# Two column pieces per held output tile: the end of a retention and feed-forward kernel on one core

## The chip, the cores and the metric

The kernel runs on one core of a Trainium2 chip. The metric is the device time of one execution in microseconds (us). Before the change the median of three runs is 618.58 us, from 618.2 to 619.4.

## The reference

A block-wise retention (attention with decay) over q, k, v of 2 x 8 heads x 768 positions x 64 gives x of 1536 tokens x 512. Two feed-forward layers follow:

```python
    x = np.ascontiguousarray(attn_out.transpose(0, 2, 1, 3)).reshape(B * S, H * D)
    h = x @ w_in
    g = np.where(h >= 1, h, np.where(h <= -1, 0.0, (h + 1) ** 2 / 4))
    x = g @ w_out
    return (x @ w_a * (x @ w_b)) @ w_out2
```

w_in is 512 x 2048, w_a and w_b are 512 x 1536, and the last matrix is 1536 x 512. The change concerns the end of that last product alone.

## The kernel before, in words

Tokens are worked on in three blocks of 512 (nb = 0, 1, 2). All large products go through `mm3` (line 354): every operand is kept as a rounded high part and a low part, both in float32r, and a product of one 128-wide slice is three matmuls (high x high, high x low, low x high) that add into one PSUM bank of 128 x 512 f32. Each matmul has its own load of 128 x 128 weights before it.

The second layer runs over six groups g of 256 hidden features, two feature tiles (`fts`) each. For each group `both_banks` makes the products of x with w_a and w_b and multiplies them, and `o_stage` (line 509) then multiplies with the last matrix: for each of the four row tiles m = 0 to 3 of a token block it calls `o_bank` (line 489), which issues 2 x 3 = 6 matmuls of 512 columns. For the blocks nb = 0 and 1, and for m = 0 of nb = 2, the sum over the groups is kept in SBUF: `gather` (line 464) adds the bank to it on VectorE, and the last group's sum is stored as a whole from the SP queue (line 499). For m = 1, 2, 3 of nb = 2 three PSUM banks are set aside, so that the sum stays in PSUM over all six groups:

```python
    for m in range(1, KT):
        held[m] = banks.popleft()
```

The last call of the kernel is `o_stage(groups - 1, 2, 2)` (line 662). There TensorE has the six matmuls of m = 0, then those of m = 1, 2, 3; VectorE adds m = 0; then each held bank goes out in two halves of 256 columns: VectorE copies the first into an SBUF buffer `o` and SP's queue stores it, ScalarE copies the second and its own queue stores that (lines 504 to 507). Nothing is left to do on any engine after m = 3 but its copies and stores.

The program is written out in the order in which each engine executes it; there is no planner that reorders. The framework places the waits (semaphores) between engines from what each instruction reads and writes. An engine takes its instructions in order, so that an instruction that waits holds up all that is behind it on its engine.

Of the kernel before, what the change touches and what calls it, by code (L numbers as in the profile page):

```python
# [22 lines left out]
DM = H * D  # L23
# [12 lines left out]
def retention_ffn_kernel(ctx: ExitStack, tc: tile.TileContext, lam, att, w1i, w1o, w2ab, w2o, out):  # L36
# [7 lines left out]
    nc = tc.nc  # L44
# [16 lines left out]
    def bank():  # L61
        banks.rotate(-1)
        return banks[-1]
# [3 lines left out]
    def t2(name):  # L67
        return two.popleft()
# [282 lines left out]
            bg()  # L351


    def mm3(ps, pairs, start=True, stop=True):
        n = len(pairs)
        for i, (l, r) in enumerate(pairs):
            for j, (a, b) in enumerate(((0, 0), (0, 1), (1, 0))):
                nc.tensor.matmul(out=ps, lhsT=l[a], rhs=r[b],   # L358
                                 start=(start and i == 0 and j == 0), stop=(stop and i == n - 1 and j == 2))

    def product_in(kind, ft, nb):

        ps = bank()
        w, x = wt[kind, ft], xy[nb]
        mm3(ps, [([w[:, a, k * 128:(k + 1) * 128] for a in range(2)], [x[k][:, b] for b in range(2)])
                 for k in range(KT)])
        return ps
# [45 lines left out]
    def both_banks(ft):  # L413
# [7 lines left out]
        def prod(w, x):  # L421
            ps = bank()
            mm3(ps, list(zip(w, x)))
            return ps
# [33 lines left out]
    def gather(total, ps, first):  # L458

        if first:  # L460
            total = t2("acc")
            nc.scalar.copy(total, ps)
        else:
            nc.vector.tensor_tensor(out=total, in0=total, in1=ps, op=ALU.add)  # L464
        return total

    def y_bank(g, nb, m, last):
        ps = bank()
        fts = range(4 * g, 4 * g + 4)
        mm3(ps, [([wt["1o", f][:, a, m * 128:(m + 1) * 128] for a in range(2)],  # L470
                  [gt[1, f, nb][:, b, :] for b in range(2)]) for f in fts])
        y = acc["y", nb, m] = gather(acc.get(("y", nb, m)), ps, g == 0)
        if last:
            xy[nb] = [block[nb][:, k] for k in range(KT)]
            if nb != 1 or m >= 2:
                split_act(y, xy[nb][m][:, 0], xy[nb][m][:, 1])
            if nb == 2:
                free2(acc.pop(("y", nb, m)))
# [8 lines left out]
    held = {}  # L487

    def o_bank(g, nb, m, last):
        fts = range(2 * g, 2 * g + 2)  # L490
        r0 = nb * TB + m * 128
        pairs = [([gt[2, f, nb][:, a, m * 128:(m + 1) * 128] for a in range(2)],
                  [wt["2o", f][:, b] for b in range(2)]) for f in fts]
        if m not in held or nb < NB - 1:
            ps = bank()
            mm3(ps, pairs)
            o = acc["o", nb, m] = gather(acc.get(("o", nb, m)), ps, g == 0)
            if last:
                nc.sync.dma_start(out=out[r0:r0 + 128], in_=o)
            return  # L500
        mm3(held[m], pairs, g == 0, last)
        if last:
            o = t2("o")
            for i, copy, queue in ((0, nc.vector.tensor_copy, nc.sync), (1, nc.scalar.copy, nc.scalar)):
                cols = slice(i * DM // 2, (i + 1) * DM // 2)
                copy(o[:, cols], held[m][:, cols])
                queue.dma_start(out=out[r0:r0 + 128, cols], in_=o[:, cols])

    def o_stage(g, nb, pieces):
        last = g == FF2 // 256 - 1  # L510
        for m in range(KT):
            o_bank(g, nb, m, last)
            bg(pieces)
        for f in range(2 * g, 2 * g + 2):
            four.append(gt.pop((2, f, nb)))
            if nb == NB - 1:
                four.append(wt.pop(("2o", f)))
# [113 lines left out]
    for i in range(2, len(stages)):  # L631
        g, nb = stages[i]
# [76 lines left out]
```

## Time and profile before

| what | us |
|---|---|
| median of three runs (lowest, highest) | 618.58 (618.2, 619.4) |
| span of the profiled execution, its only given time | 618.3 |
| TensorE busy | 597.7 (97%) |
| VectorE busy | 457.3 (74%) |
| GpSimd busy | 278.5 (45%) |
| ScalarE busy | 267.8 (43%) |

One execution was profiled. Busy time is the sum of the spans of an engine's instructions; matmuls are pipelined and their ends are modelled, so two that follow each other overlap in the records, and the distance of their starts is what one costs. In the profile PE is TensorE (PEld its weight loads), DVE VectorE, ACT ScalarE, POOL GpSimd, and SPq and ACTq are the DMA issues of SyncE and ScalarE. The page's chain follows the work that ended last back from the end, at each step to what released it. Tiles have the names of the program: `ps` is a PSUM bank, `four` and `late_four` are split operands, `two` and `late_two` are 128 x 512 f32 buffers in SBUF, which `o` is one of.

### The profile page before, as it was taken

How to read it: one execution, taken by the hardware profiler on the slowest of the kernel's cores; microseconds unless marked ns; L12 is line 12 of the kernel's file. 1: busy time of each engine (PE TensorE's matmuls, PEld its weight loads, DVE VectorE, ACT ScalarE, POOL GpSimd, SP SyncE). 2: the span in 40 equal slices, each digit the busy share in tenths (PEclk: the TensorE clock that was granted, in tenths of full speed). 3: DMA queues.
4: the chain of work that ended last, by engine and by line, in shares of the span. 5: the costliest groups of instructions: out<-in, count | busy, mean ns of one | idle time of the engine just before them, and what ended most of it. 6: DMA issues, size and time to landing. Idle time of an engine off the chain costs nothing.

```text
span 618.3 us, 8380 instructions
## 1 busy us (share of the span) xinstructions
PE 597.7 (97%) x3100; PEld 488.4 (79%) x3100; DVE 457.3 (74%) x684; ACT 267.8 (43%) x473; POOL 278.5 (45%) x218
## 2 busy tenths in 40 slices
PE   7797899999999999999999999999999999999997
PEld 3676678888888888888888788888888888888886
DVE  1578861964975786497869997989979979979553
ACT  1245552655642553264545456434424424424110
POOL 3535570443522543352947655553453553543420
PEclk9799899999999999999999999999999999999999
DMA  5965520221310212131101222302302202300004
GB/s 176 378 247 203 184 92 1 75 96 68 103 64 10 98 68 69 34 103 49 55 1 35 68 87 83 103 34 90 95 21 96 92 18 93 100 14 1 0 23 182
DMA packets 20937, 52.72 MB, mean 85 GB/s; under 512 B 2584, under 2 KB 4896, under 8 KB 20896
## 3 DMA queue, kind: packets, MB, share of 16 engines
q1 hardware_dynamic: 19624, 51.52, 24.3%
q10 hardware_dynamic: 1272, 0.67, 0.4%
q8 instruction: 24, 0.39, 0.3%
q14 instruction: 17, 0.14, 0.1%
HBM read 49.03 MB, written 3.15 MB: 84 GB/s over the span
## 4 chain that ended last, share of the span: by engine, by line
PE 82%; DVE 8%; ACT 4%; POOL 2%; issue 2%; DMA 1%; ACTq 0%; DVEq 0%; POOLq 0%
PE ps L358 79%; DVE words L294 1%; PE ps L225 1%; PE ps L221 1%; DVE two L302 1%; DVE words L298 1%; DVE two L401 1%; DMA lamp<-in_lam 1%; ACT words L280 1%; DVE two L311 1%; PE ps L150 1%; DVE two L180 1%; DMA rows<-base 1%; ACT four L265 1%; ACT two L281 0%
## 5 line engine op out<-in xcount | busy, mean ns | idle before, releaser
L266 POOL TENSOR_TENSOR four<-two,four 128x512 fp32r<-128x512 f32 x109 | 143.1, 1319 | 213.6 <-ACT four L265 203.4
L358 PE MATMUL ps<-block,four 128*128 128x512 f32 x828 | 196.9, 391 | 1.4 <-POOL block L266 1.4
L358 PEld LDWEIGHTS ps<-block,four 128*128 128x128 f32 x828 | 154.6, 188 | 35.4 <-POOL block L266 1.8
L358 PE MATMUL ps<-four,four 128*128 128x512 f32 x633 | 162.0, 389 | 0.0
L358 PEld LDWEIGHTS ps<-four,four 128*128 128x128 f32 x633 | 118.7, 188 | 24.9 <-issue 0.2
L265 ACT CAST four<-two 128x512 fp32r<-128x512 f32 x109 | 67.1, 620 | 93.4 <-DVE two L451 23.7
L266 POOL TENSOR_TENSOR late_four<-two,late_four 128x512 fp32r<-128x512 f32 x47 | 62.2, 1329 | 56.8 <-ACT late_four L265 49.5
L358 PE MATMUL ps<-block,late_four 128*128 128x512 f32 x324 | 77.2, 389 | 0.0
L358 PEld LDWEIGHTS ps<-block,late_four 128*128 128x128 f32 x324 | 60.8, 188 | 12.6
L280 ACT ACTIVATE words<-raw 128x512 f32<-128x512 f32 x68 | 43.1, 634 | 55.0 <-DVE two L302 49.7
L358 PE MATMUL ps<-four,late_four 128*128 128x512 f32 x243 | 64.0, 389 | 0.0
L377 ACT ACTIVATE two<-two,half 128x512 f32<-128x512 f32 x42 | 30.2, 720 | 70.4 <-DVE two L376 70.4
L294 DVE TENSOR_SCALAR words<-words 128x512 f32<-128x512 f32 x68 | 47.0, 691 | 17.4 <-ACT words L280 17.4
L358 PE MATMUL ps<-late_four,four 128*128 128x512 f32 x213 | 58.5, 389 | 0.0
L358 PEld LDWEIGHTS ps<-four,late_four 128*128 128x128 f32 x243 | 45.6, 188 | 9.5
L464 DVE TENSOR_TENSOR two<-two,ps 128x512 f32<-128x512 f32 x62 | 42.2, 680 | 13.1 <-PE ps L358 13.1
L311 DVE CUSTOM_DVE_ANT_0 two<-two,two 128x1024 uint16<-128x1024 uint16 x54 | 49.7, 921 | 1.9
L376 DVE TENSOR_SCALAR two<-ps 128x512 f32<-128x512 f32 x42 | 28.7, 684 | 29.9 <-PE ps L358 29.4
L298 DVE TENSOR_SCALAR words<-words 128x512 int32<-128x512 int32 x68 | 47.5, 699 | 2.3
L426 DVE TENSOR_TENSOR two<-two,ps 128x512 f32<-128x512 f32 x50 | 32.9, 682 | 19.2 <-PE ps L358 16.7
L358 PEld LDWEIGHTS ps<-late_four,four 128*128 128x128 f32 x213 | 40.0, 188 | 8.3
L265 ACT CAST late_four<-two 128x512 fp32r<-128x512 f32 x47 | 28.9, 620 | 36.4 <-DVE two L440 11.4
(99 smaller groups left out, 596.3 us busy)
## 6 DMA issues: line engine op xcount, KB each, us to landing
load<-in_att SPq DMA_DIRECT2D x48, 256.0 KB, 5.3
raw<-in_w2ab SPq DMA_DIRECT2D x24, 512.0 KB, 3.2
raw<-in_w1i SPq DMA_DIRECT2D x16, 512.0 KB, 3.4
raw<-in_w1o SPq DMA_DIRECT2D x16, 512.0 KB, 3.3
raw<-in_w2o SPq DMA_DIRECT2D x12, 512.0 KB, 3.2
out<-two SPq DMA_DIRECT2D x7, 256.0 KB, 2.0
dmask<-rows SPq DMA_DIRECT2D x2, 256.0 KB, 4.6
out<-late_two SPq DMA_DIRECT2D x2, 256.0 KB, 2.0
```

The lines of the kernel that those rows point to most:

```text
L150: nc.tensor.matmul(out=sc[c][h % 2][:, pr * CH:(pr + 1) * CH], lhsT=kT[p0:p0 + 64, pr * CH:(pr + 1) * CH], rhs=qT[p0:p0 + 64, pr * CH:(pr ...
L265: nc.scalar.copy(hi, src)
L266: (engine or nc.gpsimd).tensor_tensor(out=lo, in0=src, in1=hi.bitcast(F32), op=ALU.subtract)
L280: nc.scalar.activation(out=words, in_=r[:, :, 1].bitcast(F32), func=ACTF.Abs)
L294: nc.vector.tensor_scalar(out=words, in0=words, scalar1=HIGH_MIN, scalar2=HIGH_MAX, op0=ALU.max, op1=ALU.min)
L298: nc.vector.tensor_scalar(out=word, in0=word, scalar1=3, scalar2=0x3FFFFFFF, op0=ALU.logical_shift_left, op1=ALU.bitwise_and)
L311: nc.vector.tensor_tensor(out=v, in0=v, in1=c, op=ALU.add)
L358: nc.tensor.matmul(out=ps, lhsT=l[a], rhs=r[b], start=(start and i == 0 and j == 0), stop=(stop and i == n - 1 and j == 2))
L376: nc.vector.tensor_scalar(out=r, in0=ps, scalar1=-1.0, scalar2=1.0, op0=ALU.max, op1=ALU.min)
L377: nc.scalar.activation(out=r, in_=r, func=ACTF.Square, scale=0.5, bias=half)
L426: add = lambda o, x, ps: nc.vector.tensor_tensor(out=o, in0=x, in1=ps, op=ALU.add)
L464: nc.vector.tensor_tensor(out=total, in0=total, in1=ps, op=ALU.add)
```

## The change

For the held tiles of the last group the six matmuls of 512 columns are replaced by two runs of six: first over the first columns of the bank, then over the rest. For m = 1 the pieces are 256 and 256 columns wide, for m = 2 and 3 they are 384 and 128. The copy and the store of a piece stand right behind its matmuls in the program: VectorE and SP's queue for the first piece, ScalarE and its queue for the second. The groups before the last are issued as they were. `skip_group_check` is an option of the program's builder and issues nothing.

```diff
-    def mm3(ps, pairs, start=True, stop=True):
+    def mm3(ps, pairs, start=True, stop=True, **kw):
...
-                                 start=(start and i == 0 and j == 0), stop=(stop and i == n - 1 and j == 2))
+                                 start=(start and i == 0 and j == 0), stop=(stop and i == n - 1 and j == 2), **kw)
...
-        mm3(held[m], pairs, g == 0, last)
-        if last:
-            o = t2("o")
-            for i, copy, queue in ((0, nc.vector.tensor_copy, nc.sync), (1, nc.scalar.copy, nc.scalar)):
-                cols = slice(i * DM // 2, (i + 1) * DM // 2)
-                copy(o[:, cols], held[m][:, cols])
-                queue.dma_start(out=out[r0:r0 + 128, cols], in_=o[:, cols])
+        if not last:
+            mm3(held[m], pairs, g == 0, False)
+            return
+        o = t2("o")
+        at0 = 0
+        for i, width in enumerate({1: (256, 256)}.get(m, (384, 128))):
+            cols = slice(at0, at0 + width)
+            at0 += width
+            mm3(held[m][:, cols], [(l, [r[b][:, cols] for b in range(2)]) for l, r in pairs],
+                False, True, skip_group_check=i > 0)
+            copy, queue = ((nc.vector.tensor_copy, nc.sync), (nc.scalar.copy, nc.scalar))[i]
+            copy(o[:, cols], held[m][:, cols])
+            queue.dma_start(out=out[r0:r0 + 128, cols], in_=o[:, cols])
```

## Rows read from the trace of the kernel before

**Rows 1.** The core: span in us and mean granted TensorE clock.

```profile
core 0: 618.3 us, clock 0.991
```

**Rows 2.** The page's chain that ended last: shares of the span by line.

```profile
PE ps L358 79%; DVE words L294 1%; PE ps L225 1%; PE ps L221 1%; DVE two L302 1%; DVE words L298 1%; DVE two L401 1%; DMA lamp<-in_lam 1%; ACT words L280 1%; DVE two L311 1%; PE ps L150 1%; DVE two L180 1%; DMA rows<-base 1%; ACT four L265 1%; ACT two L281 0%
```

**Rows 3.** The chain in order of time from 609: start us, us, what.

```profile
609.00 5.68 PE ps L358 x25
```

**Rows 4.** Timeline, TensorE: start us, us, line, form, xcount; m = 3 alone.

```profile
613.14 0.84 PE L358 MATMUL ps<-late_four,four 128*128 128x512 f32 x3
613.82 0.84 PE L358 MATMUL ps<-four,four 128*128 128x512 f32 x3
```

**Rows 5.** Timeline from 610.5, other engines; in brackets the idle time before and its releaser.

```profile
610.62 0.69 DVE L464 TENSOR_TENSOR two<-two,ps 128x512 f32<-128x512 f32 x1 [0.68 <-PE ps L358]
...
613.41 0.42 DVE L506 COPY two<-ps 128x256 f32<-128x256 f32 x1 [0.94 <-PE ps L358]
...
613.86 1.66 SPq L507 DMA_DIRECT2D out<-two  x2
613.87 0.37 ACT L506 COPY two<-ps 128x256 f32<-128x256 f32 x1 [0.99 <-DVE two L506]
...
614.70 0.42 DVE L506 COPY two<-ps 128x256 f32<-128x256 f32 x1 [0.87 <-PE ps L358]
615.16 0.37 ACT L506 COPY two<-ps 128x256 f32<-128x256 f32 x1 [0.92 <-DVE two L506]
615.56 0.34 ACTq L507 DMA_DIRECT2D out<-two  x1
```

**Rows 6.** Groups of instructions, 610 to 619: busy us, mean ns of one, idle before.

```profile
L358 PE MATMUL ps<-four,four 128*128 128x512 f32 x12 | 3.4, 389 | 0.0
...
L506 DVE COPY two<-ps 128x256 f32<-128x256 f32 x2 | 0.8, 424 | 1.8 <-PE ps L358 1.8
L506 ACT COPY two<-ps 128x256 f32<-128x256 f32 x2 | 0.7, 372 | 1.9 <-DVE two L506 1.9
```

**Rows 7.** Groups of the whole span: 512 columns out of PSUM, VectorE and ScalarE.

```profile
L376 DVE TENSOR_SCALAR two<-ps 128x512 f32<-128x512 f32 x42 | 28.7, 684 | 29.9 <-PE ps L358 29.4 <-POOL block L266 0.6
...
L428 ACT COPY two<-ps 128x512 f32<-128x512 f32 x10 | 5.8, 582 | 5.5 <-PE ps L358 5.5
```

**Rows 8.** Timeline: VectorE's masks, and the weight loads that wait for the second.

```profile
52.44 1.28 DVE L180 TENSOR_TENSOR two<-ps,dmask 128x512 f32<-128x512 f32 x2
...
53.77 0.31 PEld L225 LDWEIGHTS ps<-two,load 128*64 128x64 f32 x6
```

**Rows 9.** Two weight loads after a wait (timeline), and the group of one.

```profile
56.95 0.30 PEld L358 LDWEIGHTS ps<-block,four 128*128 128x128 f32 x2
...
L358 PEld LDWEIGHTS ps<-four,four 128*128 128x128 f32 x10 | 1.9, 188 | 0.4
```

**Rows 10.** Matmuls of 128 columns: timeline, and ns min/median/max of the line.

```profile
28.91 1.09 PE L225 MATMUL ps<-two,load 128*64 128x128 f32 x16
...
L225 PE MATMUL ps<-two,load x192: 272/273/475, 18.2 to 95.2; 128*64 128x128 f32 x192
```

**Rows 11.** Stores of the last 18 us: xcount, KB each, median us to landing.

```profile
out<-two SPq DMA_DIRECT2D x7, 256.0 KB, 2.0
...
out<-two ACTq DMA_DIRECT2D x2, 128.0 KB, 1.7
```

**Rows 12.** Windows: us, busy by engine PE PEld DVE ACT POOL, PEclk, DMA share, GB/s.

```profile
54.00:58.00 4.00, 2.52 (x34) 1.83 (x31) 3.88 (x6) 1.08 (x2) 3.53 (x3) 1.00 0.82 305
...
62.00:66.00 4.00, 1.23 (x12) 1.23 (x14) 3.84 (x6) 1.88 (x4) 2.72 (x4) 0.79 0.58 176
66.00:68.00 2.00, 2.00 (x22) 1.67 (x20) 1.75 (x3) 0.80 (x2) 1.26 (x1) 0.56 0.90 295
```

**Rows 13.** Timeline of TensorE: the longest idle time before the second clock drop.

```profile
64.77 1.97 PE L221 MATMUL ps<-two,st 64*64 64x128 f32 x16 [4.62 <-POOL two L172]
```

## The prediction

> **What bounds the kernel now.** I read first the clock of the core [rows 1], then the chain that ended last on the page [rows 2], then the same chain over the last nine microseconds [rows 3], and then the last stage instruction by instruction. The chain is TensorE's line 358 for 79% of the span, at a clock of 0.991; so nearly every microsecond that TensorE stands still is a microsecond of the kernel. In the last stage TensorE is one unbroken piece until 614.68, then come a VectorE copy, a ScalarE copy, and the last store. This stage is all that the change touches: the products of earlier groups into held banks are issued as before, and taking the output buffer a little earlier costs nothing, since no engine issues anything for it.
>
> Each of the four output tiles has six matmuls here. Tile m=3 is the last two rows of TensorE's timeline, three matmuls each, which begin at 613.14 and 613.82; so one matmul of 512 columns costs 0.68/3 = 0.227 us and a tile 1.36 [rows 4]. Of these, 512 columns at 2.4 GHz are 0.213, so some 0.014 is spent per matmul. After the last tile's first matmul (613.14) VectorE starts its copy 1.56 later, ScalarE its copy 2.02 later, and the last store is issued 2.42 later, at 615.56 [rows 5]. The store lands 1.7 later, at 617.3, and 1.0 us of closing work ends the span at 618.3.
>
> The row that decides is ScalarE's copy. It reads other columns of the bank than VectorE's copy and writes other columns of the output buffer, yet in both rows it starts 0.03 to 0.04 us after VectorE's ends, and the bracket of its row names VectorE as the releaser [rows 5]. It is not the output buffer that makes it wait: at 613.87 it writes that buffer while the store issued from it at 613.86 has just begun, and does not wait for that. What the two copies share beyond it is the PSUM bank. I read from this that the program orders accesses of different engines to a bank by bank, not by columns.
>
> **The change, part by part.** For each held tile it puts 12 matmuls in place of 6: six on the first columns (piece A), six on the rest (piece B). Between them stands VectorE's copy of A. If the bank is the unit of order, B's first matmul writes the bank that this copy is reading, so it waits for the copy; TensorE takes its work in order, so the next tile's matmuls wait behind it. The cover that hid the copy in the kernel before (the next tile's six matmuls) is gone, three times.
>
> The length of the stall, by rows. The last matmul of a 512-column tile is modelled at 0.389 and VectorE starts 0.04 after its end (613.82 + 0.84 = 614.66, to 614.70) [rows 4 to 6]; for 256 columns I take 0.389 less 0.107 for the missing columns, 0.28; for 384 columns 0.34. VectorE's copy of 256 columns takes 0.424 [rows 6]; of 512 columns out of PSUM an operation takes 0.684, so 384 columns come to 0.55, half way [rows 7]. ScalarE takes 0.372 for 256 [rows 6] and 0.582 for 512 [rows 7], so 0.27 for 128. From the end of a VectorE operation to the weight load that waited for it I find 0.05 (53.72 to 53.77) [rows 8]. One full weight load keeps the following load waiting 0.30 - 0.188 = 0.11 [rows 9], and the first matmul needs its weights, so 0.11 more before B streams.
>
> A matmul of 256 columns I cost at 256/2.4 GHz + 0.014 = 0.12, of 384 at 0.174; the load's 0.11 still fits under both. Not so for 128 columns, where the stream would be 0.067 but the load needs 0.11. The trace has no such matmul: 128 columns are seen only with unrounded f32 operands and 64-wide weights, 16 in 1.09 us, (1.09 - 0.273)/15 = 0.054 each, two halves of the array in turn and two instructions for each product [rows 10]. Those share the column count, but not the operand type and not the whole array. Line 358 shares both, and bounds the cost from above at 0.227, its cost for 512 columns. The lower bound is the weight load, 0.11. The value is nearer to neither row, so I take the middle, 0.17, and keep both ends for the range. TensorE: Matmul & The Clock Gate of the Trainium skill, section Back-to-back issue gap, gives 81 ns for a sustained load and matmul of 128 columns; by that the sum below would be about 1.0 lower, at 2.4. No run here shows its figure, and for 512 columns it has 131 ns where rows 4 have 227.
>
> Counted from each tile's first matmul:
> m=1 (256+256): the last of A starts at 5 x 0.12 = 0.60, ends by the model at 0.88, VectorE starts at 0.92 and ends at 1.35 (it is free: its addition for m=0 ends at 611.31, this would start at 611.35 [rows 5]); the load comes at 1.40, B streams from 1.51, and the next tile begins 6 x 0.12 later, at 2.24. Before: 1.36. **+0.88.**
> m=2 (384+128): A's last start 0.87, end 1.21, copy 1.25 to 1.80, load 1.85, B from 1.96, next tile at 1.96 + 6 x 0.17 = 2.98. **+1.62** (0.11: +1.26; 0.227: +1.96).
> m=3: B's last matmul starts at 1.96 + 5 x 0.17 = 2.81, modelled at 0.31 (between 0.23 and 0.39), ScalarE's copy starts at 3.16, takes 0.27, and the store is issued 0.03 later, at 3.46, against 2.42. **+1.04** (+0.66; +1.41). VectorE's copy is no longer before ScalarE's here, but it has moved in front of the matmuls instead.
> Last store: 64 KB in place of 128. A store of 256 KB lands in 2.0 and one of 128 in 1.7 [rows 11]; I take **-0.1**, with -0.3 and 0 as ends. SP's larger store of m=3 is issued some 1.6 us before ScalarE's and is home first; the number of stores on each queue is unchanged.
> Sum: 0.88 + 1.62 + 1.04 - 0.1 = **+3.4** (2.7 with the narrow matmuls at 0.11, 4.1 at 0.227). On the profiled execution, whose only given time is its span, that is 618.3 + 3.4 = 621.7; this execution lies 0.3 under the median of the three runs (618.58), so the forecast is **622.0**.
>
> On the wait itself: what rows 5 show is reader against reader. PSUM — Partial Sum Buffer of the Trainium skill, section PSUM bank collisions raise a hardware error, asks for the same guard between a matmul's write and a reader, even at other columns of the bank. No row here shows that pair; by the page the sum stands as it is, and without it the first rival holds.
>
> **The rivals.**
> No slower than can be measured: B doesn't wait, because a matmul's write is ordered against a read by columns. What speaks for it is that stores and copies of one output buffer are ordered so [rows 5]. What speaks against it is ScalarE's copy, which waits with no column in common. Then m=1 costs 12 x 0.12 - 1.36 = +0.08, m=2 6 x 0.174 + 6 x 0.17 - 1.36 = +0.70, and in m=3 ScalarE would start at 1.04 + 0.85 + 0.31 + 0.04 = 2.24 and the store be issued at 2.54, +0.12; with -0.1, +0.8 in all: 619.4. With narrow matmuls at 0.11 it is +0.08 + 0.34 - 0.25 - 0.1 = +0.1: 618.7. It decides at the first matmul of B: the point is whether that starts before VectorE's copy ends.
> Slower still: the stalls let TensorE's clock fall. It did fall, from 2.4 to 1.2 GHz for a while, after TensorE had stood still for 4.62 us before 64.77 (granted 0.79 and 0.56 of full in the windows from 62 to 68); from 54 to 58, busy for 2.52 of 4 us, it was granted 1.00 throughout [rows 12, 13]. After the change I work out idle gaps under 0.8 us in the timeline, with TensorE busy about three quarters of the time, so I expect no fall. If it does fall, the columns of m=2's B and m=3 cost twice: 6 x 0.17 + 6 x 0.174 + 5 x 0.17 = +2.9 at most, 624.9 at worst, near 624 if the fall comes with m=3.
> A third, within the forecast: the narrow matmuls at either end, 621.3 or 622.7.
>
> **How the numbers follow.** Forecast with its two ends 82%, B not waiting 12%, the clock falling 6%. The unknowns of the forecast are the narrow matmuls (-0.7, +0.7), the 384-column copies (0.13 each way, twice), VectorE's start after the matmuls (in the stream it is 0.11 after the modelled end, not 0.04: +0.07 three times) and the store (-0.2, +0.1): 620.8 to 623.4 if all go one way. The page's 81 ns would give 621.0. I widen that a little for launch-to-launch scatter (618.2 to 619.4) and for part of the clock's rival: **620.3 to 623.6**. About 0.2%, 1.2 us, is what a measurement of this kernel can tell from no change. Slower by more than that: the forecast, the clock, and a small part of the first rival, 88%. Within it: the rest of that rival, 10%. Faster by more would need 1.2 us out of a tail whose two copies last 0.8 together: 2%.
>
> **What would show it right or wrong.** In the timeline of the last stage: TensorE no longer one piece but with three gaps of some 0.5 to 0.8 us, each ended by VectorE's copy; the first matmul of each B just after that copy's end; six narrow matmuls in 0.7 to 1.4 us; ScalarE's last copy waiting for TensorE, not VectorE; the chain ending TensorE, VectorE, TensorE, ScalarE. The tiles' starts should lie 2.2 and 3.0 apart, not 1.36. The forecast is wrong if B's matmuls begin while VectorE still copies A, or if the granted clock is under 1.00 before the last matmul.

## The result, and the profile after

The changed kernel takes 622.12 us (median of 12 runs, 620.66 to 625.33) where the kernel before takes 618.14 (median of 12, 617.83 to 621.05). The ratio is 1.0056, with a 95% interval of 1.0038 to 1.0074: slower by 3.5 us, between 2.3 and 4.6. The lowest runs are 2.8 apart.

The last stage of the changed kernel, TensorE's timeline (start us, us, line, form, xcount, in brackets the idle time before and its releaser), where [rows 4] had the last of one unbroken piece:

```profile
612.89 0.52 PE L358 MATMUL ps<-late_four,four 128*128 128x256 f32 x3
613.25 0.52 PE L358 MATMUL ps<-four,four 128*128 128x256 f32 x3
614.35 0.62 PE L358 MATMUL ps<-late_four,four 128*128 128x256 f32 x3 [0.58 <-DVE late_two L512]
614.81 0.52 PE L358 MATMUL ps<-four,four 128*128 128x256 f32 x3
615.17 0.69 PE L358 MATMUL ps<-late_four,four 128*128 128x384 f32 x3
615.69 0.68 PE L358 MATMUL ps<-four,four 128*128 128x384 f32 x3
617.10 0.55 PE L358 MATMUL ps<-late_four,four 128*128 128x128 f32 x3 [0.72 <-DVE two L512]
617.49 0.50 PE L358 MATMUL ps<-four,four 128*128 128x128 f32 x3
617.82 0.74 PE L358 MATMUL ps<-late_four,four 128*128 128x384 f32 x3
618.40 0.69 PE L358 MATMUL ps<-four,four 128*128 128x384 f32 x3
619.74 0.55 PE L358 MATMUL ps<-late_four,four 128*128 128x128 f32 x3 [0.65 <-DVE two L512]
620.13 0.49 PE L358 MATMUL ps<-four,four 128*128 128x128 f32 x3
```

VectorE and ScalarE in the same stretch, to be held against [rows 5]:

```profile
613.10 0.69 DVE L464 TENSOR_TENSOR two<-two,ps 128x512 f32<-128x512 f32 x1 [0.67 <-PE ps L358]
613.87 0.42 DVE L512 COPY late_two<-ps 128x256 f32<-128x256 f32 x1
616.49 0.56 DVE L512 COPY two<-ps 128x384 f32<-128x384 f32 x1 [2.19 <-PE ps L358]
619.12 0.56 DVE L512 COPY two<-ps 128x384 f32<-128x384 f32 x1 [2.08 <-PE ps L358]
```

```profile
620.66 0.27 ACT L512 COPY two<-ps 128x128 f32<-128x128 f32 x1 [2.37 <-PE ps L358]
620.95 0.34 ACTq L513 DMA_DIRECT2D out<-two  x1
```

Before each second piece stands a gap, and its bracket names VectorE's copy of the first piece: the copy of 616.49 ends at 617.05, the next weight load and matmul begin at 617.10. ScalarE's last copy now waits for TensorE, where it waited for VectorE. The tiles' first matmuls lie 2.27 and 2.65 us apart (612.89, 615.17, 617.82), where they were 1.36.

The changed stretch by itself, from m=1's first matmul to the end of the span, took 618.31 - 610.42 = 7.89 us before and 623.54 - 612.89 = 10.65 after: **+2.76**. m=1 of the kernel before begins here:

```profile
610.42 0.84 PE L358 MATMUL ps<-late_four,four 128*128 128x512 f32 x3
```

The rest of the distance of the two profiled spans lies ahead of that stretch, where both kernels issue the same instructions: m=1 begins 2.47 later after the change (612.89 against 610.42). The chain of each profile (start us, us, what) shows that this distance is there in full when the attention stage ends and the long run of 984 matmuls begins, the kernel before first:

```profile
0.73 4.93 DMA lamp<-in_lam
95.51 223.28 PE ps L358 x984
```

```profile
0.73 6.48 DMA lamp<-in_lam
97.98 223.28 PE ps L358 x984
```

The first load on the chain took 1.55 longer in the execution profiled after the change, and the first 16 matmuls of line 221 on the chain began 1.48 later (23.33 against 21.85). The other 1.0 arose between them and the long run. The mean granted clock of the first 100 us was lower too (third column from the right, the kernel before first):

```profile
0.00:100.00 100.00, 84.47 (x840) 64.53 (x841) 59.30 (x100) 42.12 (x90) 47.51 (x44) 0.95 0.57 198
```

```profile
0.00:100.00 100.00, 83.02 (x829) 63.65 (x830) 59.41 (x100) 41.62 (x89) 47.29 (x44) 0.90 0.57 198
```

The mean clock alone does not order the executions: the reordered kernel below, again with the same instructions up to there and granted 0.95 in its first 100 us, came to its m=1 at 608.34, and the kernel with other widths, which has the change's code but for the widths, at 608.60. So this distance is one between executions, and no run ties it to the change; what sets it was not found. I compare the experiments by this end stretch, and give the runs' times beside it.

### The profile page after: what moved, and what is told of

Read it like the earlier page. It is cut to its first block, busy times and chain, and to the rows that moved or that the text cites. A ratio compares the mean times of both kernels' runs of the same rounds, so it can differ in the third digit from the quotient of the medians.

```text
span 623.5 us, 8419 instructions
## 1 busy us (share of the span) xinstructions
PE 600.2 (96%) x3118; PEld 491.1 (79%) x3118; DVE 457.8 (73%) x684; ACT 267.6 (43%) x473; POOL 278.3 (45%) x218
## 4 chain that ended last, share of the span: by engine, by line
PE 83%; DVE 7%; ACT 3%; POOL 3%; issue 2%; DMA 2%; ACTq 0%; DVEq 0%; POOLq 0%
PE ps L358 79%; PE ps L225 1%; PE ps L221 1%; DMA lamp<-in_lam 1%; DVE words L294 1%; PE ps L150 1%; DVE two L401 1%; ACT words L280 1%; DVE two L302 1%; DVE words L298 1%; POOL two L172 1%; POOL four L266 1%; DMA rows<-base 1%; ACT four L265 1%; POOL two L161 0%
## 5 line engine op out<-in xcount | busy, mean ns | idle before, releaser
L358 PE MATMUL ps<-four,four 128*128 128x512 f32 (+2 forms) x642 | 162.8, 387 | 0.0
L358 PE MATMUL ps<-late_four,four 128*128 128x512 f32 (+3 forms) x222 | 59.6, 383 | 2.0 <-DVE two L512 1.4
```

The costliest lines, as they stand in the source:

```text
L358: nc.tensor.matmul(out=ps, lhsT=l[a], rhs=r[b], start=(start and i == 0 and j == 0), stop=(stop and i == n - 1 and j == 2), **kw)
```

## The experiments

All kernels leave everything ahead of the last call of `o_stage` as it is, unless told. "End stretch" is the time from m=1's first matmul to the end of the span: 7.89 before, 10.65 after.

**The copies behind both pieces.** The matmuls of the change, without their wait (here and below, code is cut to the lines that matter):

```diff
+        for i, cols in enumerate(pieces):
             mm3(held[m][:, cols], [(l, [r[b][:, cols] for b in range(2)]) for l, r in pairs],
                 False, True, skip_group_check=i > 0)
+        for i, cols in enumerate(pieces):
             copy, queue = ((nc.vector.tensor_copy, nc.sync), (nc.scalar.copy, nc.scalar))[i]
             copy(o[:, cols], held[m][:, cols])
...
```

> The same twelve matmuls per held tile, of 256+256 and 384+128 columns, but both copies stand behind the second piece, so no matmul can wait for a copy. Theory (the price is TensorE's wait for VectorE's copy): only the extra matmul time is left, with the times of the changed kernel's profile +0.07 us in m=1, +0.35 in m=2 and +0.38 up to the last store's issue, less 0.15 for the smaller store: +0.65 us over the kernel before, within 0.2% of it, 2.1 us under the changed kernel; no idle time of TensorE in the last stage. Rival (the narrow matmuls and their weight loads are the price, and the wait would have been spent anyhow): no gain on the changed kernel, +2.8 us over the kernel before.

Measured: end stretch 8.77, +0.88 on the kernel before and 1.88 below the change. Ratio to before 1.0019 (1.0003 to 1.0034); lowest run 618.91 against 618.02. No matmul waits. The waits of this stretch (who waited for whom: us in total, times, longest) are of one copy for the other and for TensorE only, as before the change:

```profile
ACT late_two L512 <- DVE late_two L512: 12.1, 1, 12.1
ACT two L512 <- DVE two L512: 2.8, 2, 1.4
DVE two L512 <- PE ps L358: 2.3, 2, 1.2
DVE late_two L512 <- PE ps L358: 0.8, 1, 0.8
```

The theory holds: two thirds of the price is the wait. The remainder is 0.23 above what I expected. The matmuls and copies came to +0.77 up to the last store's issue (expected +0.80). The store accounts for the miss: from its issue to the end of SP's wait for all stores it took 1.86, not 1.60 as in the change, though it is just as small. SP's store of 192 KB had been issued 0.27 before it here, 1.21 before it in the change; that this is the reason is likely, and taken up at the end.

**First pieces first.** The same instructions in another order: first piece A of m=1, 2, 3 (`part` is 0), then piece B of each, every piece with its copy and store behind it:

```diff
+        i = part
+        cols = slice(0, widths[0]) if i == 0 else slice(widths[0], DM)
...
+        if last and nb == NB - 1:
+            for m in held:
+                o_bank(g, nb, m, last, 1)
```

> The first pieces of m=1, 2, 3 one after the other, then their second pieces, each piece copied and stored at once as in the change. The same matmuls, copies and stores, only the order differs. Theory: each first piece's copy lies beside another bank's matmuls, so no matmul waits; twelve runs of matmuls take 4.83 us in place of 4.08, the last copy and store are 0.7 us shorter: +0.05 us against the kernel before (same within 0.2%), 2.7 us under the changed kernel. Rival (TensorE stands still because of the narrow form itself or of its weight loads, whatever bank is read): the gaps stay, +2.8 us over the kernel before.

Measured: end stretch 8.20; ratio to before 1.0008 (0.9990 to 1.0026); lowest run 618.33 against 618.02. Most of the loss is gone with not one matmul, copy or store less than in the change. TensorE is one piece again, while VectorE copies the last two wide pieces:

```profile
610.10 0.68 PE L358 MATMUL ps<-late_four,four 128*128 128x384 f32 x3
610.62 0.68 PE L358 MATMUL ps<-four,four 128*128 128x384 f32 x3
611.14 0.52 PE L358 MATMUL ps<-late_four,four 128*128 128x256 f32 x3
611.49 0.52 PE L358 MATMUL ps<-four,four 128*128 128x256 f32 x3
```

```profile
610.37 0.56 DVE L513 COPY two<-ps 128x384 f32<-128x384 f32 x1 [0.62 <-PE ps L358]
611.34 0.56 DVE L513 COPY two<-ps 128x384 f32<-128x384 f32 x1 [0.41 <-PE ps L358]
```

It is 0.26 worse than expected (7.89 + 0.05 = 7.94). ScalarE's timeline shows where: its three copies and stores now come close together, and each copy starts only after the issue of the store before it:

```profile
612.92 0.27 ACT L513 COPY two<-ps 128x128 f32<-128x128 f32 x1 [0.50 <-PE ps L358]
613.22 0.34 ACTq L514 DMA_DIRECT2D out<-two  x1
613.66 0.27 ACT L513 COPY two<-ps 128x128 f32<-128x128 f32 x1 [0.47 <-PE ps L358]
```

TensorE's last matmul ends at 613.30, so the last copy could have begun at 613.34; it began at 613.66, after the issue that ended at 613.56. The bracket names TensorE, which had been done for 0.36 us: here it is not the releaser.

**Other widths.**

```diff
-        for i, width in enumerate({1: (256, 256)}.get(m, (384, 128))):
+        for i, width in enumerate({1: (256, 256), 2: (448, 64), 3: (256, 256)}[m]):
```

> The changed kernel with other widths: m=1 256+256, m=2 448+64, m=3 256+256. Theory (a matmul under about 256 columns costs its weight load, 0.11 us): the 64-column matmuls start 0.11 us apart like those of 128 columns; the 448-column ones 0.20; m=2 takes 2.86 us, and from m=3's first matmul to the last store's issue 2.82 (3.13 in the changed kernel). Rival (a matmul costs its columns plus 0.014): the 64-column matmuls start 0.04 us apart and m=2 takes 2.4 us. Both: three gaps of TensorE, each as long as VectorE's copy plus some 0.1 to 0.2.

Measured: 64-column matmuls start 0.11 us apart (three of them from 613.40 to 613.73), as those of 128 columns do in the change (617.49 to 617.82, above); m=2 takes 2.86 (610.87 to 613.73):

```profile
610.87 0.77 PE L358 MATMUL ps<-late_four,four 128*128 128x448 f32 x3
611.48 0.78 PE L358 MATMUL ps<-four,four 128*128 128x448 f32 x3
613.04 0.52 PE L358 MATMUL ps<-late_four,four 128*128 128x64 f32 x3 [0.79 <-DVE two L512]
613.40 0.50 PE L358 MATMUL ps<-four,four 128*128 128x64 f32 x3
613.73 0.48 PE L358 MATMUL ps<-late_four,four 128*128 128x256 f32 x2
```

At 64 and 128 columns the cost of a matmul does not follow its columns; it stays at the 0.11 for which a weight load keeps the next one waiting [rows 9]. That the load sets it, and not another fixed cost of each matmul, is inferred from this agreement: no run changes the load alone. From m=3's first matmul to the last store's issue it is 2.89 (expected 2.82, 3.13 in the change). End stretch 10.74, one run, 621.15.

**One tile alone.**

```diff
+        if m != 1:
+            mm3(held[m], pairs, False, True)
+        for i, cols in enumerate(pieces):
+            if m == 1:
...
```

Here m=2 and 3 are multiplied whole and copied in halves as before the change; m=1 alone has its two pieces.

> One part of the change alone: m=1 is split into 256+256 columns, m=2 and m=3 are as in the kernel before. Theory (the price is one wait and its extra matmul time for each split tile, and they add up): m=1 takes 2.27 us in place of 1.36, and from m=1's first matmul to the end of the span it is 7.89 + 0.91 = 8.80 us. Rival (a gap is made good later, since the tail behind it has slack): under 8.2 us.

Measured: m=1 takes 2.28 us and the end stretch 8.82, +0.93: the gap is not made good behind it. One run, 620.19.

**Two banks in one tile, then two tiles.** My reading was that the program keeps the order by bank. In the first of two kernels m=3's pieces lie in two banks of one PSUM tile, A in `pair[:, 0]` and B in `pair[:, 1]`; before that, the two banks are buffers like the five others:

```diff
-    banks = deque(ps_p.tile([128, 512], F32, name=f"ps{i}") for i in range(7))
+    banks = deque(ps_p.tile([128, 512], F32, name=f"ps{i}") for i in range(5))
+    pair = ps_p.tile([128, 2, 512], F32, name="pair")
+    banks.extend((pair[:, 0], pair[:, 1]))
```

> The changed kernel, but the sum of m=3 lies in two banks of one PSUM tile: its first 384 columns in one bank, its last 128 in the other. For that its products are cut in two in all six groups, and one bank fewer is left for the other products, so that the time as a whole says little (some 1.8 us more before the last stage, or above that). Theory (the order is kept by bank): in the last stage m=1 and m=2 have their gaps of 0.59 and 0.72 us as in the changed kernel, and m=3 has none: the first narrow matmul starts 0.17 after the last wide one, while VectorE still copies, and from m=3's first matmul to the last store's issue it is 2.2 us in place of 3.13. Rival (the order is kept by tile): m=3 keeps its gap of 0.65.

Measured: the rival. m=3 keeps its gap although its pieces share no bank:

```profile
666.84 0.68 PE L362 MATMUL pair<-four,four 128*128 128x384 f32 x3
668.17 0.55 PE L362 MATMUL pair<-late_four,four 128*128 128x128 f32 x3 [0.65 <-DVE two L517]
```

```profile
667.56 0.56 DVE L517 COPY two<-pair 128x384 f32<-128x384 f32 x1 [2.09 <-PE pair L362]
```

The second kernel gives B a tile of its own (`rest = banks.popleft()`):

> As the kernel with two banks in one tile, but the two banks of m=3 are two PSUM tiles. Its products are cut in two in all six groups here too, and three banks are left for the other products. Theory (after that kernel: the program keeps the order by PSUM tile, not by bank and not by columns): in the last stage m=3 has no gap; its first narrow matmul starts 0.17 us after the last wide one, VectorE's copy of the wide piece lies beside the narrow matmuls, and from m=3's first matmul to the last store's issue it is 2.2 us in place of 3.14; m=1 and m=2 keep their gaps. Rival (a matmul waits for the last copy issued before it, whatever it reads): the gap of 0.65 stays in m=3. For the time as a whole: if the one tile was what cost the 55 us of that kernel, this one is within 1 to 6 us of the changed kernel; if the missing bank was, it stays above 660.

Measured: no gap. The first narrow matmul starts 0.17 after the last wide one and 0.20 before VectorE's copy of the wide piece, which then runs beside the narrow ones; m=1 and m=2 keep their gaps:

```profile
623.70 0.55 PE L358 MATMUL ps<-late_four,four 128*128 128x128 f32 x3 [0.72 <-DVE two L512]
...
624.42 0.75 PE L358 MATMUL ps<-late_four,four 128*128 128x384 f32 x3
625.00 0.68 PE L358 MATMUL ps<-four,four 128*128 128x384 f32 x3
625.52 0.45 PE L358 MATMUL ps<-late_four,four 128*128 128x128 f32 x3
625.81 0.49 PE L358 MATMUL ps<-four,four 128*128 128x128 f32 x3
```

```profile
625.72 0.56 DVE L512 COPY two<-ps 128x384 f32<-128x384 f32 x1 [2.08 <-PE ps L358]
```

From m=3's first matmul to the last store's issue it is 2.22 as expected, against 3.13. As a whole the two kernels take 675.31 and 631.98, one run each, and neither of my two guesses on the second was met: of some 57 us over the kernel before, 43 go with the one tile, in which alone the two kernels differ, and the other 14 with the cut products of all groups and the missing bank. How these 14 divide stays open.

**The last tile's wide piece early, and a store moved.** Order m=1, A of m=3, m=2, B of m=3, so that only one tile is cut and its copy lies beside m=2's matmuls:

```diff
-        for m in range(KT):
+        final = last and nb == NB - 1
+        for m in (0, 1, 3, 2) if final else range(KT):
             o_bank(g, nb, m, last)
...
+        if final:
+            o_bank(g, nb, 3, last, 1)
```

> Order m=1, first 384 columns of m=3, m=2, last 128 columns of m=3. m=1 and m=2 have six matmuls of 512 columns again and are copied in halves (m=2: ScalarE first, VectorE second). Theory: the copy of m=3's first piece is hidden behind m=2's matmuls, no matmul waits, the weight-load-bound pieces add 0.35 us, and the end after the last matmul is 0.7 us shorter: 0.3 to 0.4 us under the kernel before, too little for the clock on the wall (same within 0.2%) but to be seen in the profile, from m=1's first matmul to the end of the span 7.5 us against 7.89. Rival: a gap of TensorE stays before the last piece, at least 0.5 us, and it is no better than the kernel before.

Measured: no gap before the last piece, but an end stretch of 7.94; ratio to before 1.0011 (0.9995 to 1.0027), lowest run 618.12 against 618.02. TensorE did what was expected; the gain went elsewhere. ScalarE's last copy, 0.23 late, stands behind the issue of m=2's store (its bracket names VectorE's copy of m=2's other half, which ended just before it too; the next kernel tells the two apart):

```profile
614.54 0.34 ACTq L519 DMA_DIRECT2D out<-two  x1
614.98 0.27 ACT L518 COPY two<-ps 128x128 f32<-128x128 f32 x1 [0.47 <-DVE two L518]
```

The second kernel issues that store from SP's queue:

```diff
-            queue.dma_start(out=out[r0:r0 + 128, cols], in_=o[:, cols])
+            (nc.sync if m == 2 else queue).dma_start(out=out[r0:r0 + 128, cols], in_=o[:, cols])
```

> The kernel with the order m=1, first piece of m=3, m=2, last piece of m=3, but the store of the half of m=2 that ScalarE copies is issued from SP's queue. Theory (ScalarE's last copy came late because its sequencer was issuing a store for 0.34 us): that copy starts 0.04 after the last matmul's modelled end, not 0.26, and from m=1's first matmul to the end of the span it is 7.65 us against 7.93 in that kernel and 7.89 in the kernel before; the lowest run some 0.2 under the lowest of the kernel before, same within 0.2%. Rival (the copy waited for VectorE's copy of the same bank or for something else): it starts 0.26 after the matmul's end as before, 7.9 us.

Measured: the copy starts 0.04 after the matmuls' end, while VectorE's copy of m=2's half still runs (612.78 to 613.20), so the issue was what held it; the last store is issued 4.93 after m=1's first matmul, against 5.15 in the kernel before this one and 5.14 before the change:

```profile
612.46 0.49 PE L358 MATMUL ps<-four,four 128*128 128x128 f32 x3
```

```profile
612.78 0.42 DVE L518 COPY two<-ps 128x256 f32<-128x256 f32 x1 [1.17 <-ACT two L518]
```

```profile
613.00 0.27 ACT L518 COPY two<-ps 128x128 f32<-128x128 f32 x1 [0.24 <-PE ps L358]
613.29 0.35 ACTq L519 DMA_DIRECT2D out<-two  x1
```

But the end stretch is 7.97, not 7.65. SP issues its two stores of 128 KB at 612.78 and 613.24, and all stores are home only 1.98 after the last issue, where a last store of 64 KB with none issued in the 0.7 us before it took 1.60 (the change, and the kernel with the first pieces first). Ratio to before 1.0002 (0.9986 to 1.0017), lowest run 618.07 against 617.89: the same as the kernel before. No order of these pieces that I tried beats it.

## Why the prediction was right, and which step was off

The forecast was 622.0, in the range 620.3 to 623.6, and 622.12 was measured. That the median falls so near is partly luck: the sum was 0.64 too high and the median before the change was taken 0.44 too high (618.58 for 618.14), and 1.2 from outside the changed stretch makes up for both. The terms tell more:

| term | forecast | with the narrow matmul at 0.11 | profile |
|---|---|---|---|
| m=1 | +0.88 | +0.88 | +0.91 |
| m=2 | +1.62 | +1.26 | +1.29 |
| m=3 to the last store's issue | +1.04 | +0.66 | +0.71 |
| last store | -0.1 | -0.1 | -0.15 |
| sum | +3.4 | +2.7 | +2.76 |

- **The wait** came where it was placed, three times, with idle times of 0.58, 0.72 and 0.65 (0.5 to 0.8 were forecast). That it is the larger part of the price, and not the cut as such, is shown by the copies behind both pieces (-1.88) and by the reordered pieces (-2.45).
- **What orders the accesses** was read one step too far. ScalarE waiting for VectorE at other columns [rows 5] was taken to mean the bank. A tile of two banks waits just so, two tiles do not: the waits that the framework places go by PSUM tile. As each held tile was one bank the sum came out the same. PSUM — Partial Sum Buffer of the Trainium skill, section PSUM bank collisions raise a hardware error, asks for a guard by bank. Whether two tiles in one bank would be kept apart was not tried.
- **The narrow matmul** is the term that was mis-sized: 0.17, the middle of two bounds, where 0.11 was measured, the lower one. The 64-column pieces, at the same 0.11, show that it is not the columns that cost it; the weight load is what fits (see other widths). By the formula in TensorE: Matmul & The Clock Gate of the Trainium skill, section LDWEIGHTS (loading the stationary operand), a load of 128 columns is estimated at 128/1.2 = 107 ns. The 112 ns measured here agree with that within 5. The same page of the Trainium skill, section Back-to-back issue gap, has 81 ns for a sustained load and matmul of 128 columns, by which the forecast's sum was 2.4. This kernel does not show that figure (112 ns, and a sum of 2.76).
- **The tail**: VectorE's copy of 384 columns, 0.558, and ScalarE's of 128, 0.266, were worked out at 0.55 and 0.27. VectorE was not quite free for its first copy, as had been reckoned: its addition for m=0 ended only at 613.78, and the copy began 0.98 after m=1's first matmul, not 0.92. The closing work after the last landing is 1.0 as before.
- **The rivals.** That B does not wait is out by the gaps. The clock did not fall: from 612.9 to 620.7 it was granted 1.00, with TensorE busy for 5.77 of 7.80 us, 74% (three quarters were forecast).

```profile
612.90:620.70 7.80, 5.77 (x37) 4.78 (x35) 2.23 (x4) 0.68 (x3) 0.00 (x0) 1.00 0.39 139
```

- **The rest of the 4.0 us between the medians**, 1.2, is not in the changed stretch. The lowest runs lie 2.83 apart, close to the stretch's 2.76. The two profiled executions differ ahead of it, in the first load and in the attention stage, as shown above; the other executions were not profiled. Whether the change makes the longer runs more frequent was not settled. The upper end "if all go one way" adds up to 623.3, not 623.4, which changes nothing in the range. One more step of the prediction was wrong here without harm: an execution's own time is 1.8 us over its span (625.33 for 623.5), so that the execution profiled before lay some 1.5 over the median of its runs, not 0.3 under it.

## What to carry to other kernels

Before a product is cut so that its first part can leave early, look for what the copy of that part will stop: with both parts in one PSUM tile the second part's matmuls wait for the copy, and all work behind them with it. Put another tile's matmuls between the parts, or give the parts tiles of their own; here the first only came level with the kernel before, and the second cost more elsewhere than the gap. Do not cut below the width at which a matmul stops getting cheaper (here 0.11 us: 256 columns still cost 0.12, 128 cost 0.11; by the forecast's columns/2.4 GHz + 0.014 an estimate of some 235), and count the store issues on the queue of the engine that makes the last copy.

## What the runs showed that I had not expected

- A copy on ScalarE starts only after the issue of the store before it in that engine's order: 0.34 us of its sequencer, which moved the last copy by 0.2 to 0.3 us in two kernels and went away in the one where SP issued the store instead.
- In these profiles the last landing went with the stores issued just before it: 64 KB took 1.60 us with no other store in the 0.7 us before it, 1.73 with one of 128 KB issued 0.28 earlier (the kernel with the last tile's wide piece early) and 1.86 with one of 192 KB issued 0.27 earlier; with two of 128 KB issued 0.51 and 0.05 earlier all were home after 1.98. The size counts too: 128 KB with no store just before it took 1.73 (the kernel with other widths).
- A PSUM tile of two banks used as two rotating buffers cost tens of microseconds against single ones (675.31 and 631.98, one run each).
